# Linear attention and a two-layer network on one core: q and k transposed by half chunk, late keys against late queries only

## The chip, the core and the metric

The kernel runs on one core of a Trainium2 chip, with TensorE (PE), VectorE (DVE), ScalarE (ACT), GpSimd (POOL) and SyncE (SP), and 16 DMA engines behind the queues of SP and POOL. The metric is device time in microseconds. The kernel before was run three times: 177.3, 177.74 and 178.73 us, median 177.74.

## The reference

A decaying attention state per head, and a network of two layers behind it:

```python
# q, k, v, alpha: (4, 8, 768, 48) float32, alpha in 0.8 to 1
for t in range(S):
    state = alpha[:, :, t, :, None] * state + einsum('bhd,bhe->bhde', k[:, :, t], v[:, :, t])
    y[:, :, t] = einsum('bhd,bhde->bhe', q[:, :, t], state)
x = y.transpose(0, 2, 1, 3).reshape(B * S, H * D)        # 3072 x 384
h = x @ w_in                                             # 384 x 2048
out = square(maximum(h, 0)) @ w_out                      # 2048 x 384
```

## The kernel before

The 3072 rows are worked as 12 pairs, each of two chunks of 128 rows (256 rows; three pairs per batch). Rows lie in SBUF two to a partition: partition p of a chunk pair holds rows 2p and 2p+1 (the index `n`, or `i` in loads), so 64 partitions hold one chunk.

Attention of one pair goes in these stages.
- `loads` (L591): alpha, k, q, v, 384 KB each, by SP's queue (pair 2 by POOL's).
- `decay` (L621): logarithms of alpha on ACT, running sums over the rows by matmuls with a triangle (L637), exponentials, and the scaling of k and q by them on DVE into `qks` (L658, two instructions of 128x768). `values` (L612) casts v to bf16 into `vbf` on ACT.
- The scaled q and k are transposed into `qkt`: for pairs 0 to 3 on PE, for pairs 4 to 11 by one DMA transpose of 128 x 2048 elements (`turned_dma`, L718).
- `scores` (L759): 32 matmuls on 64x64 tiles of PE, each with 128 columns of queries, into four PSUM banks. All keys of a chunk meet all its queries; the triangle is cut out by four maskings of 128x512 on DVE into `pm` (L780).
- `carry` (L788): k times v for the state behind each chunk, 32 (or 16) small matmuls, an addition on DVE (L817), and a multiplication with the decay on POOL (L819) into `sbf`.
- For pairs 4 to 11 `mixed_back` (L897): 32 matmuls of masked scores with values (L920, 64x128 tiles, so 128 rows of output at once), and the queries with the state of before in two groups of 8 or 16 (L910, 64x64 tiles). The second waits until the first has left PE; work of another kind is put between. ACT copies the result to `yb`, and a second DMA transpose on SP (L939) makes `xt`, the network's input. Pairs 0 to 3 get `xt` from PE directly (`mixed`, L826).

The network: `up` (L953) makes 256 of the 2048 middle columns for a pair by six matmuls (L963), eight such steps a pair; ACT applies the relu (L973), DVE squares (L975). `down` (L989) has four steps of four matmuls (L996) for each chunk, then an evacuation on ACT and `store` (L942). In pairs 4 to 10 the rows come out with even and odd rows in the two halves of the partitions, and two DMAs of 64 partitions on POOL put them back for each chunk. A few matmuls on zeros (L982) fill PE while it waits at the start.

The order is not that of the code. Every step is added with a place from `TABLE` (in units of a pair's half), and `Program.order` (L147) simulates the five engines and two queues with costs given by hand, and always takes the ready instruction with the lowest place. The result is a fixed program for each engine, with waits on semaphores between them. An engine does its program in order, so one late instruction holds all behind it.

Of the kernel before, what the change touches and what calls it, by code (L numbers as in the profile page):

```python
# [16 lines left out]
    dict(decay0=-101.63878, decay1=-64.79031, turned0=-73.57009, turned1=-62.54519, scores0=-30.02735, scores1=-46.13048, carry=-24.00248, mixed=-12.61483, up=3.82089, down=9.97184, scale00=37.96521, scale01=12.07767, scale10=-55.27694, scale11=66.26176, ends=3.96969, values=3.22532, loads=-198.59615),  # L17
    dict(decay0=-62.3532, decay1=-43.34947, turned0=-42.30728, turned1=-37.91382, scores0=-25.93696, scores1=-11.6373, carry=-24.1783, mixed=3.23949, up=7.51554, down=6.63429, scale00=34.30537, scale01=-58.35352, scale10=17.21724, scale11=40.27209, ends=44.67154, values=2.77668, loads=-199.72423),
    dict(decay=-3.52293, turned=6.45487, scores0=6.82966, scores1=6.65956, carry=-0.27539, mixed=10.50945, up=12.79282, down=3.90935, loads=-64.41188),
    dict(decay=7.24503, turned=8.97861, scores0=9.08238, scores1=9.71941, carry=9.32967, mixed=10.63684, up=15.57323, down=2.06012, loads=-61.40619),  # L20
    dict(decay=7.93117, turned=8.88166, scores0=11.15836, scores1=10.85679, carry=9.32967, mixed=11.76255, up=15.22484, down=2.29842, loads=-62.88919),
    dict(decay=8.06004, turned=10.03837, scores0=11.3686, scores1=10.90735, carry=10.59388, mixed=11.41181, up=16.11414, down=1.46618, loads=5.03271),
    dict(decay=7.68334, turned=10.80342, scores0=11.5973, scores1=11.84935, carry=10.99201, mixed=14.31953, up=16.37508, down=1.46618, loads=5.21441),
    dict(decay=11.20522, turned=12.7234, scores0=13.91124, scores1=13.85916, carry=12.42083, mixed=14.21671, up=16.27226, down=1.75528, loads=11.16392),
    dict(decay=11.49025, turned=11.82737, scores0=13.75226, scores1=14.7438, carry=12.85879, mixed=15.63875, up=17.67473, down=1.71467, loads=9.89433),
    dict(decay=11.5844, turned=11.68949, scores0=14.67671, scores1=14.63718, carry=14.26836, mixed=15.50289, up=17.56635, down=1.71467, loads=9.53939),
    dict(decay=10.86409, turned=12.68953, scores0=16.09372, scores1=14.63718, carry=14.3971, mixed=11.80752, up=17.60364, down=1.71467, loads=10.75129, masks=-31.23894),
    dict(decay=10.86409, turned=12.68953, scores0=15.58331, scores1=14.80708, carry=14.3971, mixed=15.0505, up=17.60364, down=1.71467, loads=10.84157),
]
POOLS = [dict(decay=0, turned=2, scores=2, carry=1, mixed=2), dict(decay=2, turned=2, scores=1, carry=0, mixed=1)]  # L30
WEIGHTS = (-75.69063, -62.43345)
TURNED = (0, 1, 2, 3)
BACK = (4, 5, 6, 7, 8, 9, 10, 11)
BEHIND = {6: 4, 7: 6, 8: 6, 9: 7, 10: 7, 11: 9}
RUNS = {10: 16}
WARMUP = (28, 1)
WIDE = 0
PARTS = ((1, 3, 6), (2, -1, 3))
OPENS = {3: 7}
QUEUED = (2,)  # L40
# [19 lines left out]
class Program:  # L60
# [26 lines left out]
    @classmethod  # L87
    def kind(cls, eng, dma, nbytes):
        if dma in ("turn", "back"):
            return cls.TURN, 1000.0, 800.0, 256.0  # L90
        if dma[0] == "w":
            return 0.0, 2450.0, 1350.0, nbytes / 384.0 if dma[1] == "i" else 1536.0
        if dma[:3] == "raw":
            return cls.PAIR, 1100.0 if eng == "SP" else 2450.0, 1100.0, 350.0
        return cls.ROWS, 1000.0, 900.0, 1536.0
# [330 lines left out]
def bass_gla_recurrent__then__act_relu_squared_kernel(  # L426
# [32 lines left out]
    NY, NX = 2, 6  # L459
    NGT, NRR, NOS = 3, 4, 8  # L460
# [13 lines left out]
    VBF = sb("vbf", [128, 2, H, PAD], BF16, NV)  # L474
    SBF = sb("sbf", [128, D + NP * PAD], BF16, NS)
# [8 lines left out]
    MASK = sb("mask", [128, 2, 2, 64], BF16)  # L484
    WIN = sb("win", [128, KT, DFF], BF16)
# [3 lines left out]
    OSB = sb("osb", [128, DM], FP32, NOS)  # L489
# [45 lines left out]
    for c in range(2):  # L535

        add("POOL", lambda g, c=c: g.affine_select(
            out=MASK[64 * c:64 * c + 64], in_=MASK[64 * c:64 * c + 64], compare_op=ALU.is_ge, fill=0.0,
            base=0, pattern=[[-1, 2], [1, 2], [2, 64]], channel_multiplier=-2),
            470, -6, reads=["mask"], writes=["mask"])  # L540
    for i in range(NQK):
# [49 lines left out]
    def loads(g, at):  # L591
        b, t0, r = g // NW, (g % NW) * TW, g % NRAW
        for j, src in ((3, alpha), (0, k), (1, q), (2, v)):
# [5 lines left out]
            if g in QUEUED:  # L599
# [11 lines left out]

    def values(g, at):  # L612
        r, vb = g % NRAW, g % NV
        dst, src = VBF[vb][:, :, :, 0:D], both(r, 2)
# [6 lines left out]
    def decay(g, at):  # L621
# [34 lines left out]
        for z in range(2):  # L656
            decays = bass.AP(tensor=ASB[a], offset=z * 2 * HD, ap=[[4 * HD, 128], [0, 2], [D, H], [1, D]])
            add("DVE", lambda dve, z=z, decays=decays: dve.tensor_tensor(  # L658
# [59 lines left out]
    def turned_dma(g, at):  # L718
        x, t = g % NQK, g % NQT
        dst = QKT[t][:].rearrange("p z i j s -> p (z i j) s")  # L720
# [37 lines left out]

    def scores(g, at, js=range(NP), late=0.0):  # L759
        t, m = g % NQT, g % NPM  # L760
        halves = sorted({j // 2 for j in js})
        banks = {(i, X): bank(POOLS[g]["scores"] if g < FIRST else 0) for X in halves for i in range(2)}

# [24 lines left out]
    def carry(g, at, spots=None):  # L788
        x, vb, c_ = g % NQK, g % NV, g % NAC
# [4 lines left out]
        def mm(pe):  # L794
            for j in range(NP):
                for n in range(2):
                    for i in range(2):
                        for c in chunks:
                            last = pe.matmul(banks[c][0][64 * i:64 * i + 64, j * D:(j + 1) * D],  # L799
                                             QKS[x][64 * c:64 * c + 64, 0, n, 2 * j + i, :],  # L800
                                             VBF[vb][64 * c:64 * c + 64, n, 2 * j + i, 0:D],
                                             start=n == 0, stop=n == 1)
            return last
        add("PE", mm, 250, at, reads=[("qks", x, 0, X) for X in range(2)] + [("vbf", vb)],
# [21 lines left out]
    def mixed(g, at, spots=None, between=None):  # L826
# [42 lines left out]
        reads = [("qkt", t, 1, X) for X in range(2)] + [("sbf", (2 * g + c) % NS) for c in chunks]  # L869
# [27 lines left out]
    def mixed_back(g, at, spots=None, between=None):  # L897

        t, m, vb, b_ = g % NQT, g % NPM, g % NV, g % NY
        banks = [pr.bank(spots or shared) for c in range(2)]  # L900
        chunks = [1] if g % NW == 0 else [0, 1]

        def before(pe, swap):
            for j in range(NP):
                for i in range(2):
                    c = i ^ swap
                    for n in range(2):
                        if c in chunks:
                            h = 2 * j + i
                            last = pe.matmul(banks[c][0][64 * n:64 * n + 64, D * h:D * h + D],  # L910
                                             QKT[t][64 * i:64 * i + 64, 1, n, j, 64 * c:64 * c + 64],
                                             SBF[(2 * g + c) % NS][64 * i:64 * i + 64, D + PAD * j:2 * D + PAD * j],
                                             start=False, stop=True, skip_group_check=True)
            return last

        def mm(pe):
            for h in range(H):
                for i in range(2):
                    for c in range(2):
                        last = pe.matmul(banks[c][0][:, D * h:D * h + D], PMB[m][64 * c:64 * c + 64, h % 2, h // 2, i, :],  # L920
# [189 lines left out]
    for g in QUEUED:  # L1110
        ahead(("weights", g - 2), [("loads", g)])
# [64 lines left out]
```

## Time and profile before

| | |
|---|---|
| profiled execution, its time | 177.66 us |
| its span on the core | 175.9 us |
| TensorE clock granted | 1.00 |
| DVE, ACT, POOL busy | 120.3, 116.8, 38.5 us |
| read from HBM, written | 25.17, 4.72 MB |
| the chain that ended last, by engine | PE 85%, DMA 9% of the span |

A group row gives line, engine, operation, tiles and shapes, the number of instructions, their busy time together and the mean of one in ns, then the engine's idle time before them and what ended it. A timeline row gives start, length and the same names. A row of a source line's view gives least, median and greatest duration in ns; the row of waits gives the total, the number of times and the longest. Matmuls are pipelined: the length of a group ends with the last matmul's end, so the distance from one group's start to the next is what it costs.

### The profile page before, as it was taken

To read this page: it belongs to the slowest core of one execution; us is meant where nothing else is said; L and a number is where in the kernel's file an instruction comes from. 1 tells how busy PE (TensorE), PEld (TensorE's weight loads), DVE (VectorE), ACT (ScalarE), POOL (GpSimd) and SP (SyncE) were. 2 spreads that over 40 slices of the span, in tenths; PEclk is the share of its full clock that TensorE was granted. 3 is DMA by queue.
4 is the path that set the end of the run, shared out by engine and by line. 5 is a ranking of instruction groups with operands and counts; after the bars stand their busy time and mean duration, and the time that the engine had idled before them with its cause. 6 is when DMAs were issued, how large, how long until landed. Compare 5 with 4: busy or idle time off the path is not lost.

```text
span 175.9 us, 5997 instructions
## 1 busy us (share of the span) xinstructions
PE 168.3 (96%) x2609; PEld 123.8 (70%) x2609; DVE 120.3 (68%) x253; ACT 116.8 (66%) x233; POOL 38.5 (22%) x68
## 2 busy tenths in 40 slices
PE   7899598999999999999999999999999999999994
PEld 7556466766778677786777777776777777777773
DVE  7887844986899899888737939877885551232220
ACT  3884458666889677489868697767675545656641
POOL 4099820100012001010222131212330302220120
PEclk9999999999999999999999999999999999999999
DMA  5999999899996994999999989999491133212222
GB/s 146 324 294 173 203 338 221 140 276 246 318 321 100 307 304 101 148 315 201 324 201 319 238 159 296 195 321 173 100 182 32 22 71 60 56 22 48 45 45 91
DMA packets 76314, 32.89 MB, mean 187 GB/s; under 512 B 69632, under 2 KB 75456, under 8 KB 76288
## 3 DMA queue, kind: packets, MB, share of 16 engines
q1 hardware_dynamic: 70384, 25.04, 61.4%
q0 software_dynamic: 5904, 7.47, 20.7%
q8 instruction: 20, 0.33, 0.8%
q14 instruction: 6, 0.05, 0.1%
HBM read 25.17 MB, written 4.72 MB: 170 GB/s over the span
## 4 chain that ended last, share of the span: by engine, by line
PE 85%; DMA 9%; POOL 2%; ACT 1%; DVE 1%; issue 1%
PE psO L996 34%; PE psH L963 33%; DMA win<-in_moe_w_in_dram 6%; DMA xt<-yb 3%; PE psG L770 3%; PE psO L982 2%; PE psG L920 2%; POOL win L574 2%; PE psG L799 2%; PE psG L838 2%; PE psO L1015 2%; PE psG L910 1%; PE psG L710 1%; PE psG L637 1%; DVE qks L691 1%; ACT asb L688 1%
## 5 line engine op out<-in xcount | busy, mean ns | idle before, releaser
L973 ACT ACTIVATE rr<-psH 128x512 bf16<-128x512 f32 x96 | 58.2, 611 | 37.6 <-PE psH L963 36.5
L963 PE MATMUL psH<-xt,win 128*128 128x256 bf16 x576 | 75.8, 273 | 2.5 <-DMA win<-in_moe_w_in_dram 2.1
L996 PE MATMUL psO<-wout,gt 128*128 128x384 bf16 x368 | 71.5, 326 | 0.7 <-ACT xt L879 0.7
L975 DVE TENSOR_TENSOR gt<-rr 128x512 bf16<-128x512 bf16 x96 | 41.4, 439 | 38.4 <-ACT rr L973 37.9
L963 PEld LDWEIGHTS psH<-xt,win 128*128 128x128 bf16 x576 | 54.0, 98 | 16.1 <-ACT rr L973 3.1
L996 PEld LDWEIGHTS psO<-wout,gt 128*128 128x128 bf16 x368 | 35.0, 98 | 17.3 <-ACT xt L879 0.9
L949 POOL DMA_DIRECT2D out_dram<-osb x28 | 15.1, 544 | 71.3 <-ACT osb L1003 71.0
L780 DVE TENSOR_TENSOR pm<-psG,mask 128x512 bf16<-128x512 f32 x45 | 28.7, 682 | 1.8 <-PE psG L770 0.6
L819 POOL TENSOR_TENSOR sbf<-ust,acp 128x192 bf16<-128x192 f32 x16 | 9.3, 580 | 52.4 <-DVE ust L817 52.3
L658 DVE TENSOR_TENSOR qks<-raw,asb 128x768 bf16<-128x768 f32 x20 | 18.3, 951 | 3.2 <-ACT asb L647 3.2
L1003 ACT ACTIVATE osb<-psO 128x384 f32<-128x384 f32 x23 | 11.4, 494 | 3.7 <-PE psO L996 3.2
L647 ACT ACTIVATE asb<-psG 128x384 bf16<-128x384 f32 x20 | 9.8, 492 | 2.9 <-PE psG L639 2.6
L627 DVE TENSOR_TENSOR raw<-raw 128x384 f32<-128x384 f32 x20 | 11.0, 564 | 0.1
L770 PEld LDWEIGHTS psG<-qkt 64*64 64x64 bf16 x360 | 6.0, 106 | 4.3 <-issue 2.7
L770 PE MATMUL psG<-qkt 64*64 64x128 bf16 x360 | 8.7, 220 | 0.1
L619 ACT ACTIVATE vbf<-raw 128x768 bf16<-128x768 f32 x10 | 8.5, 853 | 0.2 <-DMA raw<-in_v_dram 0.2
L936 ACT ACTIVATE yb<-psG 128x384 bf16<-128x384 f32 x14 | 6.4, 490 | 2.5 <-PE psG L910 1.8
L982 PE MATMUL psO<-warm 128*128 128x128 bf16 (+1 forms) x39 | 7.0, 343 | 1.1 <-DVE warm L518 1.1
L817 DVE TENSOR_TENSOR ust<-psG,sbf 128x192 f32<-128x192 f32 x15 | 5.3, 353 | 2.5 <-PE psG L799 1.4
L627 DVE TENSOR_TENSOR raw<-raw,ro 128x384 f32<-128x384 f32 x10 | 6.1, 612 | 0.2 <-DMA raw<-in_q_dram 0.2
L643 ACT ACTIVATE ro<-raw 128x384 f32<-128x384 f32 x10 | 5.2, 518 | 0.4 <-DMA raw<-in_alpha_dram 0.4
L633 ACT ACTIVATE lab<-raw 128x384 bf16<-128x384 f32 x10 | 5.2, 524 | 0.2 <-DVE raw L627 0.2
(98 smaller groups left out, 131.0 us busy)
## 6 DMA issues: line engine op xcount, KB each, us to landing
raw<-in_alpha_dram SPq DMA_DIRECT2D x11, 384.0 KB, 4.7
raw<-in_k_dram SPq DMA_DIRECT2D x11, 384.0 KB, 4.8
raw<-in_q_dram SPq DMA_DIRECT2D x11, 384.0 KB, 4.8
raw<-in_v_dram SPq DMA_DIRECT2D x11, 384.0 KB, 5.6
out_dram<-osb POOLq DMA_DIRECT2D x28, 96.0 KB, 3.3
out_dram<-osb SPq DMA_DIRECT2D x9, 192.0 KB, 4.3
wout<-in_moe_w_out_dram POOLq DMA_DIRECT2D x4, 384.0 KB, 14.3
win<-in_moe_w_in_dram POOLq DMA_DIRECT2D x3, 384.0 KB, 9.5
```

The source lines that it names most:

```text
L627: add("DVE", lambda e: e.tensor_tensor(dst, a0, a1, ALU.mult), 470, at_, reads=reads, writes=writes, port=True)
L647: add("ACT", lambda act, z=z: act.activation(ASB[a][:, z, 0, :], ps[:, 0:HD], AF.Exp, scale=2.0 * z - 1.0), 372, at + 0.04 + 0.02 * z, rea ...
L658: add("DVE", lambda dve, z=z, decays=decays: dve.tensor_tensor(QKS[x][:, z, :, :, 0:D], both(r, z), decays, ALU.mult), 870, at + 0.05 + 0. ...
L770: last = pe.matmul(banks[i, j // 2][0][64 * c:64 * c + 64, col:col + 128].rearrange("p (a b) -> p a b", a=2), QKT[t][64 * i:64 * i + 64, 0 ...
L780: add("DVE", lambda dve, i=i, X=X, ps=ps: dve.tensor_tensor(PMB[m][:, i, 2 * X:2 * X + 2].rearrange("p j n s -> p j (n s)"), ps[:].rearran ...
L949: add(by, lambda e, dst=dst, ps=ps: e.dma_start(dst, OSB[o][ps, :]), 600, at + 0.01 * i, reads=[("osb", o)], dma=("own" if by == "POOL" el ...
L963: last = pe.matmul(ps[:, f * TW:(f + 1) * TW].rearrange("p (c t) -> p c t", c=2), WIN[:, kt, fj * 128:(fj + 1) * 128], XT[:, 2 * (g % NX): ...
L973: add("ACT", lambda act: act.activation(ro, ri, AF.Relu), 480, at, reads=[key], writes=[key, ("rr", r)])
L975: add("DVE", lambda dve: dve.tensor_tensor(gt[:, 2 * u:2 * u + 2, :], rr, rr, ALU.mult), 340, at, reads=[("rr", r)], writes=[("gt", g % NG ...
L982: last = pe.matmul(psO[1][:, 0:128 * wide].rearrange("p (a b) -> p a b", a=wide), WARM[:], bass.AP(tensor=WARM, offset=0, ap=[[128, 128], ...
L996: last = pe.matmul(ps[:, 0:DM], GT[g % NGT][:, fj, tt * 128:(tt + 1) * 128], WOUT[:, fj, :], start=(fj == 0), stop=(fj == FT - 1))
L1003: add("ACT", lambda act: act.activation(OSB[o][:], ps[:, 0:DM], AF.Copy), 372, at, reads=[key], writes=[key, ("osb", o)])
```

## The change

For pairs 4 to 11 (`turned_back(g)`):

- The scaling into `qks` writes another layout, with pairs of heads side by side, by four DVE instructions of 128x384 for two of 128x768.
- One DMA transpose becomes four, each of 32 partitions (half a chunk) of `qks`, into a quarter of `qkt`; the four are issued one behind another on SP.
- A chunk of 128 rows is seen as two halves of 64, early and late. Early keys meet all 128 queries as before (16 matmuls with 128 columns), late keys meet late queries only (16 with 64 columns). The banks hold 384 columns and not 512, and the mask `maskn` has 192 columns for 256.
- v is cast to another layout, and eight DMAs a pair, issued on POOL, copy it into `vp`, half chunk by half chunk, so that 64 partitions hold the rows of one half.
- The values are used in 64x64 tiles: 48 matmuls for 32. They and the state's 32 (16 in the first pair of a batch) are dealt into two groups: `near` (early keys, half of the state's part) and `far`.
- Two chunks are stored by four DMAs of 32 partitions, for two DMAs of 64 partitions each.
- `maskn` is made once by one memset on DVE and eight selects on POOL.

Besides, `TABLE` and the other constants are new: loads of the first two pairs can be placed in three parts, the first 13 ups (`WIDE`) take turns on three PSUM banks rather than two, pair 10's joined run is put behind another down (`RUNS`), and the pools of banks for pairs 0 and 1 differ. The places of all stages move; the kinds and numbers of ups, downs, sums, carries and of all work of pairs 0 to 3 stay.

The core of the diff:

```diff
-WIDE = 0
+WIDE = 13
...
     def turned_dma(g, at):
         x, t = g % NQK, g % NQT
+        if turned_back(g):
+            for y in range(4):
+                dst = bass.AP(tensor=QKT[t], offset=512 * y, ap=[[2048, 128], [32, 16], [1, 32]])
+                src = bass.AP(tensor=QKS[x], offset=2048 * 32 * y, ap=[[2048, 32], [1, 2048]])
+                turns[g] = add("SP", lambda sp, dst=dst, src=src: sp.dma_start_transpose(dst, src), 600, at + 0.001 * y,
...
+    def copies(g, at):
...
+        for c in range(2):
+            for a in range(2):
+                for i in range(2):
+                    to = 64 * ((a + c) % 2) + 32 * i
+                    add(COPIES, lambda e, c=c, a=a, i=i, to=to: e.dma_start(
+                        vp[to:to + 32, c, :], close(g, 64 * c + 32 * a, 32, i)), 550, at + 0.01 * (4 * c + 2 * a + i),
...
+    def scores_later(g, at, halves, banks, late):
...
+                for c in range(2):
+                    for i in range(2):
+                        ps = banks[i, j // 2][0]
+                        q = bass.AP(tensor=QKT[g % NQT], offset=2048 * 64 * i + 1024 * c + 256 + 64 * j,
+                                    ap=[[2048, 64], [512, 2], [1, 64]])
+                        o = bass.AP(tensor=ps, offset=512 * 64 * c + col, ap=[[512, 64], [64 + 64 * c, 2], [1, 64]])
+                        pe.matmul(o, part(g, 0, i, j, c, 0), q)
+                for c in range(2):
+                    for i in range(2):
+                        x = col + 64 + 64 * c
+                        last = pe.matmul(banks[i, j // 2][0][64 - 64 * c:128 - 64 * c, x:x + 64],
+                                         part(g, 0, i, j, c, 1), part(g, 1, i, j, c, 1))
...
     def mixed_back(g, at, spots=None, between=None):
...
+        def block(pe, h, c, a, b):
+
+            rows, col = 64 * ((a + c) % 2), (64 + 64 * c) * b
+            return one(pe, c, b, h, within(mn, rows, 64, h % 2)[:, h // 2, col:col + 64], vp[rows:rows + 64, c, D * h:D * h + D])
...
+        def near(pe):
+            for h in range(H):
+                for b in range(2):
+                    for c in range(2):
+                        last = block(pe, h, c, 0, b)
             for j in range(NP):
-                for i in range(2):
...
+                for a in range(2):
+                    for c in chunks:
+                        last = before(pe, j, c, c, a)
             return last
...
+        def far(pe):
             for h in range(H):
...
+                for c in range(2):
+                    last = block(pe, h, c, 1, 1)
+                for c in chunks:
+                    last = before(pe, h // 2, 1 - c, c, h % 2)
             return last
```

210 lines of the change are left out of this document (150 added, 60 removed).

## The prediction

> **What bounds the kernel now.** I read the page's busy times first, then the busy time by stretch, then the tensor engine's waits, then its timeline where pairs 4 to 11 are worked.
>
> ```profile
> PE 168.3 (96%) x2609; PEld 123.8 (70%) x2609; DVE 120.3 (68%) x253; ACT 116.8 (66%) x233; POOL 38.5 (22%) x68
> 15.00:20.00 5.00, 4.59 (x67) 3.07 (x64) 4.12 (x8) 2.50 (x5) 5.00 (x8) 1.00 1.21 195
> 20.00:25.00 5.00, 3.26 (x98) 2.57 (x99) 3.01 (x6) 2.28 (x4) 1.35 (x3) 1.00 1.19 286
> 25.00:30.00 5.00, 4.22 (x62) 2.94 (x55) 2.02 (x5) 3.33 (x8) 1.09 (x2) 1.00 1.19 254
> 40.00:50.00 10.00, 10.00 (x192) 7.33 (x190) 7.62 (x15) 7.22 (x16) 0.00 (x0) 1.00 1.06 289
> 130.00:140.00 10.00, 9.71 (x129) 7.30 (x129) 6.24 (x15) 5.86 (x10) 1.11 (x3) 1.00 0.25 47
> PE psH L963 <- DMA win<-in_moe_w_in_dram: 2.1, 3, 1.5
> PE psO L996 <- ACT xt L879: 0.7, 1, 0.7
> PE psH L963 <- DMA xt<-yb: 0.3, 1, 0.3
> ```
>
> In a stretch row the first number is its length, the second PE's busy time, and the 1.00 behind POOL's the granted clock. From 40 us on PE is full (10.00 of 10.00) but for 0.29 us after 130. Before that, the three rows from 15 to 30 us leave 0.41 + 1.74 + 0.78 = 2.93 us idle, nearly all waits for the first weights and for one evacuation. So the time is PE's own work plus a start that a transfer sets. An edit pays only where it shortens PE work, or if it opens a new gap in that full stretch, costs.
>
> **The unit costs.** One pair's attention as PE runs it (start, length, line), one row of the chain (six ups in a row of others), and three groups with the mean of one matmul:
>
> ```profile
> 69.17 0.64 PE L770 MATMUL psG<-qkt 64*64 64x128 bf16 x32
> 69.74 0.83 PE L963 MATMUL psH<-xt,win 128*128 128x256 bf16 x6
> 70.41 1.46 PE L996 MATMUL psO<-wout,gt 128*128 128x384 bf16 x8
> 71.70 1.47 PE L963 MATMUL psH<-xt,win 128*128 128x256 bf16 x12
> 73.11 0.57 PE L920 MATMUL psG<-vbf,pm 64*128 64x48 bf16 x32
> 73.61 0.31 PE L910 MATMUL psG<-sbf,qkt 64*64 64x48 bf16 x16
> 73.76 0.42 PE L799 MATMUL psG<-vbf,qks 64*64 64x48 bf16 x32
> 74.01 0.32 PE L910 MATMUL psG<-sbf,qkt 64*64 64x48 bf16 x16
> 74.27 1.48 PE L963 MATMUL psH<-xt,win 128*128 128x256 bf16 x12
> 75.68 0.64 PE L770 MATMUL psG<-qkt 64*64 64x128 bf16 x32
> 65.05 0.41 PE L799 MATMUL psG<-vbf,qks 64*64 64x48 bf16 x16
> 101.63 0.66 PE psH L963 x6
> L770 PE MATMUL psG<-qkt 64*64 64x128 bf16 x360 | 8.7, 220 | 0.1
> L799 PE MATMUL psG<-vbf,qks 64*64 64x48 bf16 x304 | 5.0, 188 | 0.0
> L920 PE MATMUL psG<-vbf,pm 64*128 64x48 bf16 x224 | 4.0, 180 | 0.0
> ```
>
> A length less one matmul's own duration is the distance from first to last start. Scores: 0.64 - 0.22 = 0.42 us for 31 steps, 13.5 ns a step. Carry, with 48 columns: 0.42 - 0.19 = 0.23 us, 7.5 ns. So a small matmul on four 64x64 tiles is cheaper when fewer columns stream through it, down to some 7.5 ns.
>
> **Scores.** Each of the eight pairs keeps 32 matmuls, but 16 of them now stream 64 columns instead of 128. No row shows 64 columns; the nearest is the 48-column carry. 16 x (13.5 - 7.5) = 0.10 us a pair; no gain is the other bound, if the mixed order doesn't pipeline. I take 0.10, as 64 is much nearer to 48 than to 128.
>
> **Values and the state's part.** Before: 0.50 us from the first L920 to the first L910, then two groups of 16 at about 7.8 ns, 0.25 us: 0.75 us, and the exits, which stay. After: 48 value blocks and 32 state blocks, all 64x64 with 48 columns, 80 x 7.8 ns = 0.62 us. That is 0.13 us less, though there are 16 matmuls more. The doubt is the second group: in half of its steps all four blocks write partitions 64 to 127, so only two tiles work. The row at 65.05 us has two tiles in use and takes 0.41 us for 16, as long as the 32 on four tiles. If what it shows is the limit of one tile, the second group takes 0.37 us instead of 0.25 and 0.12 of the 0.13 us is gone; if it is the limit of one half of the rows (those 16 all read the same 64 partitions, while the second group uses both halves), nothing is lost. L920 favours the second reading: with 0.57 - 0.18 = 0.39 us for 31 steps, 12.6 ns, it is no slower on two tiles that are twice as wide and use both halves. I take 0.13, with 0.01 as the other end.
>
> Sum: 8 x (0.10 + 0.13) = 1.84 us, between 0.1 us (neither gain comes) and 2.4 us (0.30 a pair, if the 16 shorter score matmuls and the change from wide to square tiles give 0.07 more).
>
> A rule of the Trainium skill speaks against this: "TensorE: Matmul & The Clock Gate", section "Wait — 56ns, not 53.3ns?", says that start-to-start never drops below about 25 ns however few columns there are. By that the 16 extra matmuls cost 0.4 us a pair. The trace disagrees: 7.5 ns in the carry row above.
>
> **Changes of tile shape.** Going between 128x128 and tiled work costs about 0.1 us each way: the 12 ups before the values take from 71.70 to 73.11, 1.41 us, where twice the 0.66 us of six is 1.32. The built order has 28 tiled visits after the first up where it had 27: +0.2 us.
>
> **The start.** The built order puts the second half of pair 1's scores ahead of the first up, and gives the first 13 ups a third bank. Before the last input weights land, PE has the same work to choose from, so the wait of 2.1 us moves rather than goes. Eight small selects for the new mask stand on POOL, seven ahead of a cast, one ahead of the weight loads:
>
> ```profile
> L616 POOL CAST vbf<-raw 128x768 bf16<-128x768 f32 x2 | 1.7, 862 | 4.8 <-DVE qks L691 4.8
> L525 POOL TENSOR_SCALAR_AFFINE_SELECT hinc<-hinc 128x128 bf16<-128x128 bf16 x1 | 0.3, 292 | 0.9 <-DVE hinc L523 0.9
> ```
>
> Seven times at most 0.29 us fit into the 4.8 us that the cast waits; the eighth delays the weights by up to 0.3 us. Against it stands the 0.7 us wait of L996 on an evacuated bank, which the third bank and other pools can remove. I put the start at nothing, from -1.5 to +0.5 us.
>
> **VectorE, POOL.**
>
> ```profile
> L780 DVE TENSOR_TENSOR pm<-psG,mask 128x512 bf16<-128x512 f32 x45 | 28.7, 682 | 1.8 <-PE psG L770 0.6
> L817 DVE TENSOR_TENSOR ust<-psG,sbf 128x192 f32<-128x192 f32 x15 | 5.3, 353 | 2.5 <-PE psG L799 1.4
> L658 DVE TENSOR_TENSOR qks<-raw,asb 128x768 bf16<-128x768 f32 x20 | 18.3, 951 | 3.2 <-ACT asb L647 3.2
> L691 DVE TENSOR_TENSOR qks<-raw,asb 128x384 bf16<-128x384 f32 x8 | 4.2, 552 | 0.5 <-ACT asb L688 0.5
> L949 POOL DMA_DIRECT2D out_dram<-osb x28 | 15.1, 544 | 71.3 <-ACT osb L1003 71.0
> ```
>
> A masking of 384 columns lies between 353 and 682 ns, by their slope at 550: four a pair save 0.53 us. Four scalings of 0.55 replace two of 0.95: +0.31 us. DVE is 0.2 us a pair lighter, and is no bound either way. The value copies add 8 DMA issues a pair on POOL, 64 x 0.54 = 35 us, so POOL goes from 38 to some 73 of 176 us. Behind a pair's eight issues (4.4 us) stands the multiply that makes the next state; the state is wanted by the mixing, some ten PE steps later, so I cost it at nothing, and at up to 1 us if a late ACT cast holds POOL's queue.
>
> **SyncE and the transposes.** This is where the change can lose.
>
> ```profile
> L722 SPq DMA_TRANSPOSE qkt<-qks x8: 1427/3279/3967, 54.2 to 126.6; - x8
> DMA to landing us min/median/max: 4.9/6.3/7.7
> L939 SPq DMA_TRANSPOSE xt<-yb x8: 1211/1327/3314, 66.9 to 147.2; - x8
> 126.60 2.66 SPq L722 DMA_TRANSPOSE qkt<-qks  x1
> 129.36 1.26 SPq L939 DMA_TRANSPOSE xt<-yb  x1
> 129.36 5.34 DMA xt<-yb
> ```
>
> One transpose that moves 512 KB takes SP 1.43 to 3.97 us; the smaller one, of the output, never under 1.21. Four quarters should take 4 x 1.21 = 4.84 us, 1.56 over the median, and the last lands as much later (estimate: 6.3 + 1.6 = 7.9 us). Against that the built order gives more room. Counted in ups and downs of four or six matmuls (0.65 us), there are 12, 13 and 12 between a pair's sums and its scores for pairs 4, 5 and 6 before, and 16, 20 and 17 after; the least for any of the eight goes from 12 to 14, 1.3 us more. So most of the delay is covered, and I cost it at nothing, with the bound below in the first rival. Data moved by the copies (0.2 MB a pair) and by the larger number of DMAs lies in a stretch where SP stands waiting part of the time.
>
> The profiled execution took 177.66 us, the median of the runs 177.74, so the sum needs no correction: 177.66 - 1.84 + 0.2 = 176.0 us.
>
> **The rivals.**
> *The queue of SP becomes the bound (slower).* At 126.60 a transpose of scores held SP for 2.66 us, the output transpose of pair 9 came behind it and landed 5.34 us later, and PE stood 0.25 us. After, that output transpose stands behind four quarters and a load: at least 2.2 us later (4.84 - 2.66). Pairs 4 and 10 have the same neighbourhood, with one to four quarters of the next pair ahead. If three such places each lose 1.5 us, the time is 176.0 + 4.5 = 180.5 us. It decides from some 3.6 us of new PE idle on. Against it: the wider room. The Trainium skill, "DMA: Bandwidth & Descriptors", section "Rules for kernel authors", would have small transfers coalesced, as under 64 KB mostly overhead is paid; the copies are 24 KB. No row here shows one of that size.
> *The gain is given back.* The instructions shorten but the fixed order waits instead, for masks, copies or quarters, some 0.2 us a pair: 177.7 us. For it: three waits of PE already show; against: they sum to 3 us, two thirds of it at the start.
> *The start gains too.* If half of the 2.93 us idle goes, 174.5 us.
> *Small matmuls have a floor.* If the 80 of a pair took 25 ns a step when they alternate blocks and states, 16 more cost 8 x 0.4 = 3.2 us and the time is 180.9 us. The carry row speaks plainly against it.
>
> **How the numbers follow.** The forecast has 0.46, at 176.0; its own range is 175.4 (2.4 us saved) to 177.0 (the tile limit takes 8 x 0.12 us). SP's queue 0.18, given back 0.17, start 0.15, floor 0.02, other delays 0.02. One per cent is 1.8 us, about what a measurement here can tell from no change, so 175.95 is the border. Somewhat over half of the forecast's cases lie under it (0.25), with the start 0.40 faster; the rest of it and the given-back case make 0.38; 0.22 slower. The range leaves out the floor, the upper part of SP's case and the far end of the start's: 174.0 to 179.4.
>
> **What would show it.** Right: a score group of 32 under 0.56 us from first to last end, a mixing without the gap between its two shapes, PE full from 40 us on, a mean masking of some 550 ns, the four quarters' issue near 1.2 us each. Wrong: PE waiting on the transposed q and k or on the transposed output in the middle of the span (the first rival), a second value group longer than the first per matmul (the tile limit), first ups later than 17 us (the start), or POOL's multiply held behind copies and DVE's state sum waiting on it.

## The result, and the profile after

The changed kernel takes 188.38 us (median of four runs, 186.45 to 189.24), the kernel before 177.52: 1.059 times as long, 95% interval 1.049 to 1.069. Forecast were 176.0 us, with a range up to 179.4. Times and ratios here leave out the few runs that lay more than 1.5% above the fastest of their kernel. The profiled execution took 188.35 us, 10.7 more than the 177.66 of before, and its span is 186.6 us against 175.9.

From the page, the busy times and the chain that ended last:

```profile
PE 169.5 (91%) x2741; PEld 124.6 (67%) x2741; DVE 117.7 (63%) x270; ACT 115.0 (62%) x233; POOL 73.8 (40%) x140
PE 57%; DMA 14%; DVE 9%; SPq 8%; POOL 3%; ACT 3%; issue 3%; POOLq 0%
```

PE works about as long as before (168.3 us), but only 57% of the chain is PE, where it was 85%. DMA, SP's own issuing (SPq) and DVE have come in. The next two fences are the busy time by stretch (length, then PE's busy time) and PE's waits from 40 us on:

```profile
40.00:180.00 140.00, 132.00 (x2164) 1.00 0.86 179
70.00:80.00 10.00, 8.07 (x190) 1.00 0.76 136
120.00:130.00 10.00, 8.18 (x172) 1.00 1.17 222
```

```profile
PE psG L849 <- DMA qkt<-qks: 5.7, 4, 2.0
PE psG L849 <- issue: 1.2, 1, 1.2
PE psO L1125 <- DVE gt L1103: 0.6, 1, 0.6
```

From 40 us on PE is idle for 8.0 us, where it was idle for 0.29. Nearly all of it (6.9 us) stands at L849, the first matmul of a pair's scores, and waits for the transposed q and k: the row without a releaser (issue) is one of these too, for it ends 0.09 us after pair 6's last quarter has landed. PE's last matmul ends at 181.4 us against 173.5 before: 7.9 us later, of which 7.7 are this idle time.

The remaining 2.8 us lie at the end. The closing line's instructions (duration three times, then the start), after and before:

```profile
L1274 POOLq DRAIN  x1: 9385/9385/9385, 177.0 to 177.0; - x1
L1274 SPq DRAIN  x1: 7/7/7, 183.6 to 183.6; - x1
```

```profile
L1125 POOLq DRAIN  x1: 4096/4096/4096, 168.2 to 168.2; - x1
```

Before the program ends each engine drains. GpSimd's drain took 4.1 us before and was over at 172.3, before PE was. Now it takes 9.4 us, from 177.0 to 186.4, and SP, which is done at 183.6, waits 2.8 us for it. No step of the prediction had a drain in it.

SP's side of the wait, from the timeline (start, length) and the view of one line; L787 is a quarter, L621 a load, L1060 the output transpose, L1077 a store:

```profile
57.66 3.12 SPq L787 DMA_TRANSPOSE qkt<-qks  x2
60.82 0.58 SPq L1077 DMA_DIRECT2D out_dram<-osb  x1
61.44 0.44 SPq L621 DMA_DIRECT2D raw<-in_k_dram  x1
61.93 0.68 SPq L621 DMA_DIRECT2D raw<-in_q_dram  x1
62.65 1.75 SPq L621 DMA_DIRECT2D raw<-in_v_dram  x1
64.52 5.71 SPq L787 DMA_TRANSPOSE qkt<-qks  x3
70.27 1.88 SPq L1060 DMA_TRANSPOSE xt<-yb  x1
72.20 1.29 SPq L787 DMA_TRANSPOSE qkt<-qks  x1
...
75.32 0.25 PE L849 MATMUL psG<-qkt 64*64 64x128 bf16 x4 [1.93 <-DMA qkt<-qks]
```

```profile
L787 SPq DMA_TRANSPOSE qkt<-qks x32: 1217/1291/3052, 53.9 to 147.4; - x32
DMA to landing us min/median/max: 2.7/4.1/7.2
```

Pair 5's q and k were scaled by 60.1 us. Its first quarter is issued at 64.5, since SP is still busy with pair 4's quarters, a store and three loads. Its fourth goes out at 72.2, behind an output transpose that held SP for 1.88 us (its input had been ready since 67.7), and lands at 75.27; PE starts 0.05 us later, after 1.93 us of idleness. Five of the eight pairs' scores start within 0.1 us of their last quarter's landing. Over the eight pairs the mean time from the last scaling to the last landing is 11.7 us, where it was 6.6 for one transpose. Half of the loss lies before the first issue, which now comes 2.8 us after the scaling instead of 0.3. Adding up SP's issues between 50 and 140 us gives 86.4 of 90 us (44.7 of them quarters), against 64.9 (23.7) before: SP had become full.

So two theories. **A**: four issues for one make the turned q and k late, and PE waits. **B**: the 64 copies of v that GpSimd issues lengthen its closing drain. Rivals: the new order of the work, or colliding transfers, open the gaps; the drain waits for the last stores. In the experiments "order kept" means that the fixed program of each engine is unchanged but for the edit.

### The profile page after: what moved, and what is told of

It is laid out like the page before. It is cut to its first block, busy times and chain, and to the rows that moved or that the text cites. A ratio compares the mean times of both kernels' runs of the same rounds, so it can differ in the third digit from the quotient of the medians.

```text
span 186.6 us, 6419 instructions
## 1 busy us (share of the span) xinstructions
PE 169.5 (91%) x2741; PEld 124.6 (67%) x2741; DVE 117.7 (63%) x270; ACT 115.0 (62%) x233; POOL 73.8 (40%) x140
## 4 chain that ended last, share of the span: by engine, by line
PE 57%; DMA 14%; DVE 9%; SPq 8%; POOL 3%; ACT 3%; issue 3%; POOLq 0%
PE psH L1091 24%; PE psO L1125 21%; SPq L787 7%; DMA qkt<-qks 6%; DMA win<-in_moe_w_in_dram 5%; DMA raw<-in_q_dram 3%; PE psG L1013 3%; DVE qks L717 2%; POOL maskn L553 2%; PE psO L1144 1%; PE psG L946 1%; DVE gt L1103 1%; POOL win L591 1%; PE psG L849 1%; ACT rr L1101 1%
## 5 line engine op out<-in xcount | busy, mean ns | idle before, releaser
L1101 ACT ACTIVATE rr<-psH 128x512 bf16<-128x512 f32 x91 | 54.9, 612 | 31.7 <-PE psH L1091 30.1
L1091 PE MATMUL psH<-xt,win 128*128 128x256 bf16 x546 | 70.5, 273 | 1.9 <-ACT xt L987 1.2
L1103 DVE TENSOR_TENSOR gt<-rr 128x512 bf16<-128x512 bf16 x96 | 40.3, 433 | 32.2 <-ACT rr L1101 31.9
L1091 PEld LDWEIGHTS psH<-xt,win 128*128 128x128 bf16 x546 | 51.6, 98 | 13.4 <-ACT xt L987 1.5
L652 POOL DMA_DIRECT2D vp<-vbf x64 | 31.7, 504 | 21.9 <-ACT vbf L667 20.4
L860 DVE TENSOR_TENSOR pm<-psG,maskn 128x384 bf16<-128x384 f32 x32 | 15.8, 549 | 11.6 <-PE psG L853 11.6
L717 DVE TENSOR_TENSOR qks<-raw,asb 128x384 bf16<-128x384 f32 x32 | 16.8, 580 | 1.7 <-ACT asb L702 1.7
L849 PE MATMUL psG<-qkt 64*64 64x128 bf16 x128 | 4.4, 224 | 7.0 <-DMA qkt<-qks 5.7
L849 PEld LDWEIGHTS psG<-qkt 64*64 64x64 bf16 x128 | 3.1, 106 | 9.4 <-DMA qkt<-qks 7.0
L888 DVE TENSOR_TENSOR pm<-psG,mask 128x512 bf16<-128x512 f32 x13 | 8.5, 683 | 1.0 <-PE psG L878 0.8
L1013 PE MATMUL psG<-vp,pm 64*64 64x48 bf16 x336 | 6.9, 188 | 0.0
```

Source lines behind the costliest of these rows:

```text
L652: add(COPIES, lambda e, c=c, a=a, i=i, to=to: e.dma_start(vp[to:to + 32, c, :], close(g, 64 * c + 32 * a, 32, i)), 550, at + 0.01 * (4 * c ...
L717: add("DVE", lambda dve, to=to, given=both(r, z)[:, :, y:H:2], decays=decays: dve.tensor_tensor(to, given, decays, ALU.mult), 470, at + 0. ...
L860: add("DVE", lambda dve, i=i, X=X, ps=ps: dve.tensor_tensor(within(mn, 0, 128, i)[:, 2 * X:2 * X + 2, :], ps[:, 0:384].rearrange("p (j s) ...
L1013: last = pe.matmul(banks[c][0][64 * a:64 * a + 64, D * h:D * h + D], lhsT, rhs, start=(c, a) not in begun, stop=True, skip_group_check=True)
L1091: last = pe.matmul(ps[:, f * TW:(f + 1) * TW].rearrange("p (c t) -> p c t", c=2), WIN[:, kt, fj * 128:(fj + 1) * 128], XT[:, 2 * (g % NX): ...
L1101: add("ACT", lambda act: act.activation(ro, ri, AF.Relu), 480, at, reads=[key], writes=[key, ("rr", r)])
```

## The experiments

**1. Before, with its transpose in four.** L722 issues four DMAs:

```diff
-        turns[g] = add("SP", lambda sp: sp.dma_start_transpose(dst, src), 600, at,
+        def quarters(sp):
+            for y in range(4):
+                d = bass.AP(tensor=QKT[t], offset=32 * y, ap=[[2048, 128], [128, 16], [1, 32]])
+                s = bass.AP(tensor=QKS[x], offset=2048 * 32 * y, ap=[[2048, 32], [1, 2048]])
+                last = sp.dma_start_transpose(d, s)
...
+        turns[g] = add("SP", quarters, 600, at,
```

> The kernel before with its order of instructions kept as it is; only its one transpose of q and k for each of the pairs 4 to 11 is issued as four DMA transposes of 32 partitions each, at the same place of SP's program. Theory A (four issues of about 1.3 us each, one behind the other on SP, make the turned q and k late and TensorE waits for them): SP is held 5 to 7 us for a pair instead of 1.4 to 4.0, TensorE's idle time after 40 us rises from 0.3 us to 3 us or more, the waits stand at the scores and name the DMA of qkt, and the time is 181 to 187 us against 177.5. Rival (the new order of the work, not the four issues, opened the gaps): idle time below 1 us and a time within 1 us of 177.5.

Measured: 190.9 and 192.05 us against 176.92, ratio 1.081 (1.072 to 1.090). PE's waits, and its busy time and granted clock in two stretches:

```profile
PE psG L778 <- DMA qkt<-qks: 5.2, 4, 2.7
PE psH L971 <- DMA xt<-yb: 3.5, 1, 3.5
```

```profile
80.00:85.00 5.00, 4.81 (x54) 0.66 1.06 280
135.00:140.00 5.00, 2.01 (x9) 0.57 1.00 139
```

The split alone, in the old order, costs more than the whole change. The waits stand at the scores, as theory A has it, and once at the output transpose queued behind the quarters, for 3.5 us, which is the place that the prediction's first rival named. The time is above the expected 187: PE was idle for 9.6 us after 40 us, and around the long waits the granted clock fell, which the expectation had not priced (in the two stretches shown 5 x 0.34 + 5 x 0.43 = 3.9 us; more on this below).

**2. After, with one transpose for a pair.** The first of the four moves all, the others are not issued:

```diff
-                dst = bass.AP(tensor=QKT[t], offset=512 * y, ap=[[2048, 128], [32, 16], [1, 32]])
-                src = bass.AP(tensor=QKS[x], offset=2048 * 32 * y, ap=[[2048, 32], [1, 2048]])
+                dst = QKT[t][:].rearrange("p z i j s -> p (z i j) s")
+                src = QKS[x][:].rearrange("p z i h d -> p (z i h d)")
...
         for op in self.programs[e]:
+            if op.dma in ("turn1", "turn2", "turn3"):
+                continue
```

> The changed kernel with its order kept; the first of a pair's four transposes moves the whole pair in one DMA into the same tile, the other three are left out, and the scores and the mixing read the tile at the places where they read it before. The columns then stand in another order, so q and k are mismatched and the output is not the reference's; every other instruction, wait and shape stays. Theory A: the waits on the DMA of qkt go (5.7 us in the trace of the changed kernel), TensorE's idle time after 40 us falls from 8.0 to under 2 us, its last matmul ends at about 175 instead of 181.4 us, and with the same 2.8 us of closing drain the time is 181 to 183 us. Rival (the waits come from transfers that collide, the copies and loads, whatever the number of issues): idle time stays above 6 us and the time at 187 or more.

Measured: 181.32 us, ratio 1.025 (1.018 to 1.031); 7 us of the loss are gone. No wait on qkt is left among PE's, its last matmul ends at 174.3, and the drain (9387 ns, from 170.0) ends the program. The transposes:

```profile
L790 SPq DMA_TRANSPOSE qkt<-qks x8: 1945/4098/5621, 52.9 to 135.4; - x8
DMA to landing us min/median/max: 5.0/8.1/9.3
```

One whole transpose holds SP for 4.1 us in the median where the four quarters of a pair hold it for 6.4 in the mean, and it lands after 8.1 us, slower than the 6.3 us of before. What ended the waits is thus the earlier start, on a freer SP, as much as the shorter flight. Theory A holds, by undoing (2) and by doing alone (1). With the order kept and 2.0 us of idle time left, the new order of the work is not what opens the gaps.

**3. After, without the copies.** The 64 copies are not issued, the mixing reads the tile that they would have read:

```diff
+            if op.dma is not None and op.dma[:2] == "vp":
+                continue
...
-            return one(pe, c, b, h, within(mn, rows, 64, h % 2)[:, h // 2, col:col + 64], vp[rows:rows + 64, c, D * h:D * h + D])
+            return one(pe, c, b, h, within(mn, rows, 64, h % 2)[:, h // 2, col:col + 64], bass.AP(
+                tensor=VBF[g % NV], offset=2 * H * PAD * rows + HD * c + D * h, ap=[[2 * H * PAD, 64], [1, D]]))
```

> The changed kernel with its order kept and the 64 DMA copies of v on GpSimd left out; the mixing reads v from the tile that the copies read, at addresses of the same shape, so v is in the order of the tokens and the output is not the reference's. Theory B (GpSimd's closing drain takes about 0.05 us for each DMA that the engine issued, so the 64 copies make it 9.4 instead of 4.1 us and it ends last): the drain falls to about 4 to 6 us, the end of the span follows TensorE's last matmul by about 2.3 us instead of 5.2, TensorE's idle time stays at about 8 us, and the time is 185 to 186 us. Rival (the copies' packets delay the transposes): TensorE's idle time after 40 us falls below 4 us, and the time to 181 or less. Rival (the drain waits for the last stores): drain and time unchanged.

```profile
L1291 POOLq DRAIN  x1: 4297/4297/4297, 173.8 to 173.8; - x1
```

Measured: 182.25 us, ratio 1.028 (1.023 to 1.034). The drain shrinks as theory B says. (The copies' semaphores are still there, so their number is not the cause; and the expectation's 0.05 us a DMA was too little for its own numbers, which give 5.3 us for 64.) But the gain of 6 us is twice what the drain is worth: PE's idle time after 40 us is 4.9 us and not the expected 8, and its last matmul ends at 178.1, 3.3 us earlier. Either the copies delay the transposes too, or chips differ, so it was repeated beside the changed kernel (10).

**4. After, with GpSimd's last eight stores on SP.**

```diff
+        late = self.programs["POOL"][-8:]
...
+        self.programs["POOL"] = self.programs["POOL"][:-8]
+        self.programs["SP"][-3:-3] = late
```

> The changed kernel with its order kept, but GpSimd's last eight DMAs, the stores of pairs 9 and 10, issued by SP ahead of its last three instructions. Theory B: GpSimd's drain still takes 8 us or more, since 97 DMAs of its own are left, but it begins some 10 us earlier and is hidden, and the time falls by about 2.8 us to 185 to 186 us; TensorE's idle time stays at 8 us. Rival (the drain's length is that of the last stores' landing): the drain shrinks to below 5 us. Rival (something else ends the span): time at 188 us.

```profile
L1283 POOLq DRAIN  x1: 9235/9235/9235, 150.7 to 150.7; - x1
```

Measured: 183.89 us, ratio 1.038 (1.031 to 1.044). The drain stays long, starts at 150.7 and is hidden; the last stores are not its cause. The gain of 4.5 us holds 1.6 us of an earlier end of PE, which lost 4.9 us idle and 1.7 at half clock (last section) and not the expected 8. The moved stores come behind the waits and can't give that; the changed kernel's own runs differ by as much (186.45 to 189.24 us).

**5. Before, with 64 idle copies on GpSimd.** Eight behind the last decay step of each of pairs 3 to 10:

```diff
+    def copies(eng, k):
+        for x in range(8):
+            p, c = 32 * (x % 4), x // 4
+            eng.dma_start(EXTRA[p:p + 32, k, c, :], SRC[p:p + 32, :]).then_inc(extra_sems[x], 16)
```

> The kernel before with its order kept, and 64 more DMA copies on GpSimd: after the last decay step of each of the pairs 3 to 10 eight copies of 32 partitions from one unused tile to another, 384 B for each partition, that nothing waits for but the end. Theory B (the closing drain grows with the number of copies that GpSimd issued): the drain grows from 4.1 to about 9.4 us, starts where it did, at about 168 us, and ends at about 177.6, behind SP's last wait at 175.7; the time rises by about 2 us, to 178.5 to 179.5, with TensorE's idle time after 40 us still below 1 us. Rival (the drain's length comes from the stores in four parts or from the number of semaphores): drain 4 to 5 us and time within 1 us of the kernel before. Rival (the copies' packets delay the loads and transposes): TensorE's idle time above 2 us.

```profile
L1143 POOLq DRAIN  x1: 9277/9277/9277, 167.9 to 167.9; - x1
```

Measured: 179.94 us against 177.4, ratio 1.017 (1.010 to 1.024): the drain alone, put into the kernel before, costs about what theory B says, if a little more than the expected 179.5. PE is idle for 0.8 us after 40 us, once for a transpose (0.7): here too the transposes' median hold on SP rises, from 3.28 to 3.70 us. From 4096 to 9277 ns is 81 ns a copy, though these move half the bytes of the change's. The eight stores of experiment 4 took only 150 ns off, 19 ns each. So it does not go by the number of DMAs alone, as the theory had it; why a copy within SBUF weighs more was not tried.

**6. After, planned anew with a quarter's measured price.**

```diff
-            return cls.TURN, 1000.0, 800.0, 256.0
+            return cls.TURN, 1000.0, (2500.0 if nbytes == 128 * 1024 else 800.0), 256.0
...
-                turns[g] = add("SP", lambda sp, dst=dst, src=src: sp.dma_start_transpose(dst, src), 600, at + 0.001 * y,
+                turns[g] = add("SP", lambda sp, dst=dst, src=src: sp.dma_start_transpose(dst, src), 1290, at + 0.001 * y,
```

> The changed kernel, planned anew with one correction: a quarter's transpose is told to the planner with 1290 ns on SP instead of 600, and with 2500 ns of landing instead of 800, as the trace of the changed kernel shows it. Theory A with an order that can mend it: the scores are placed later or the transposes earlier, TensorE's idle time after 40 us falls from 8.0 to under 3 us, and the time with the unchanged closing drain is 182 to 185 us. Rival (SP has too much to issue between 50 and 140 us, 96% of the time in the changed kernel, for any order to help): idle time stays above 5 us and the time at 186 or more.

Measured: 196.77 us, ratio 1.110 (1.098 to 1.122): a miss, the slowest of all. PE is idle for 10.7 us after 40 us and ran at half clock in three stretches of 3.4 us. Its longest waits are no longer for the transposes but for the logarithms (`lab`) of the decays:

```profile
PE psG L692 <- ACT lab L688: 3.8, 2, 2.2
```

So the new plan did harm in several places. SP's timeline shows one that bears on theory A:

```profile
63.10 3.98 SPq L787 DMA_TRANSPOSE qkt<-qks  x2
72.55 1.22 SPq L1060 DMA_TRANSPOSE xt<-yb  x1
73.81 2.61 SPq L787 DMA_TRANSPOSE qkt<-qks  x2
```

Two of pair 5's quarters went out, then SP stood from 67.1 to 72.5 us at an output transpose that the plan had put between them, until `yb` was written, and the other two waited behind it: 18.3 us passed from pair 5's scaling to its last landing. PE had other work meanwhile, so what this place cost is not shown. A truer price in the plan did not help where the plan may part what is wanted together.

**7. One transpose, and the late stores on SP** (2 and 4 together).

> The second and the fourth experiment in one: the changed kernel with its order kept, one transpose for a pair in place of four (columns in another order, so the output is not the reference's), and the last eight stores of GpSimd on SP. If theories A and B are the whole loss: TensorE ends at about 174.3 us as in the second experiment, the drain is hidden, and the time is 178 to 179 us, within 1.5% of the kernel before; what is left of the change then gains nothing. Rival (the end is held by something else too): 180 us or more. Rival (scores and mixing do gain once the waits are gone): 176 us or less.

Measured: 179.24 us, ratio 1.012 (1.007 to 1.017). It is a little above the expected 179; PE still stood 1.7 us in waits with no releaser shown, which are gone in experiment 12, without the copies.

**8. After, with the second value group spread over four tiles.**

```diff
                 for c in range(2):
-                    last = block(pe, h, c, 1, 1)
+                    last = block(pe, h, c, 1, 1, h // 2 % 2)
...
```

The new argument names the half of the output's partitions.

> The changed kernel, but in the second group of the mixing the blocks of late keys and late queries of every other two heads are summed into the other half of the output's partitions, so that each of the four 64x64 tiles gets 8 matmuls there instead of 12, 12, 4 and 4; the output is not the reference's. If one tile's turn of about 31 ns is the limit, the second group falls from 0.37 us to about 0.25 us for a pair. Rival (the rate at which the engine takes instructions and weights is the limit): it stays at 0.37 us.

The mixing of pair 7: in the changed kernel the first row of the first group, the first row of the second (its 32 matmuls are broken into many rows) and what follows it; then the last two in the experiment.

```profile
108.01 0.44 PE L1013 MATMUL psG<-vp,pm 64*64 64x48 bf16 x32
...
108.67 0.21 PE L1013 MATMUL psG<-vp,pm 64*64 64x48 bf16 x2
...
109.16 0.34 PE L1125 MATMUL psO<-wout,gt 128*128 128x384 bf16 x1
```

```profile
105.55 0.21 PE L1014 MATMUL psG<-vp,pm 64*64 64x48 bf16 x2
...
105.93 0.34 PE L1126 MATMUL psO<-wout,gt 128*128 128x384 bf16 x1
```

From the second group's start to the next work it was 0.49 us and is 0.38. From first to last start the 32 matmuls take 0.37 us in the changed kernel and 0.27 to 0.31 in the six pairs here that have 32 (the two first pairs of a batch have 24). The tile that gets 12 matmuls sets the time, at 31 ns each. A limit of one half of the output's partitions would fit this run too (24 of the 32 write one half in the changed kernel, 16 here), but not the prediction's row at 65.05 us: its 16 matmuls on two tiles write 8 to each half and still take 0.22 us. In one run the kernel took 186.99 us.

**9 and 10. The changed kernel again, and without copies, on one chip.**

> The changed kernel again, unaltered, so that it and the next run share a chip. Each of its runs so far had TensorE's last matmul between 179.8 and 181.4 us and a time of 186.5 to 189.2 us. If the copies play a part in the waits, this run and the next differ by more than the 2.8 us of the closing drain; if not, by that alone.

> The third experiment again (the 64 copies of v left out, so the output is not the reference's), beside the changed kernel on one chip. If the copies' packets delay the transposes: 5 us or more below the changed kernel, with TensorE's last matmul at least 2 us earlier. Rival (only the drain is theirs, and the third experiment's further gain was the spread between chips and runs): 2 to 4 us below it, TensorE's last matmul within 1 us.

Measured: 188.27 us, ratio 1.063 (1.055 to 1.072), and 182.02 us, ratio 1.027 (1.018 to 1.035), with PE's last matmul ending at 180.9 and 178.6 us. PE's longest waits with the copies, then without:

```profile
PE psG L849 <- DMA qkt<-qks: 5.1, 3, 3.0
PE psG L849 <- ACT rr L1101: 1.1, 1, 1.1
```

```profile
PE psG L708 <- ACT lab L704: 2.5, 1, 2.5
PE psG L865 <- issue: 1.5, 1, 1.5
```

The copies cost some 6 us: 2.8 in the drain, and most of the rest in PE's waits. The idle time after 40 us falls from 7.6 to 4.0 us, but behind the wait of 2.5 us the second kernel ran at half clock for 3.4 us, which gives 1.7 us back; its last matmul comes 2.3 us earlier.

**11. After, planned anew with the four transposes as one entry, late stores on SP.**

```diff
+            def quarters(sp):
+                for y in range(4):
...
+            turns[g] = add("SP", quarters, 5200, at, reads=[("qks", x, z, X) for z in range(2) for X in range(2)],
...
-            store("POOL" if turned_back(g) and g < G - 1 else "SP", o, n, at)
+            store("POOL" if turned_back(g) and g < G - 3 else "SP", o, n, at)
```

> The changed kernel planned anew with a pair's four transposes as one entry of the plan, 5200 ns on SP and 4500 ns of landing, so that nothing can be placed between them, and with the stores of pairs 8, 9 and 10 on SP. Theory A as the sixth experiment left it (four issues are dear, and dearer where SP's order puts a waiting output transpose between them): TensorE's idle time after 40 us falls below 4 us and, with the drain hidden, the time is 179 to 183 us. Rival (SP is too full for any order): 185 us or more.

```profile
PE psG L1017 <- DVE pm L864: 3.0, 2, 2.6
PE psH L1095 <- ACT rr L1105: 1.3, 3, 0.7
PE psG L853 <- DMA qkt<-qks: 0.5, 2, 0.3
```

Measured: 185.86 us, ratio 1.050 (1.044 to 1.057). That lies above the expected 179 to 183 and 2 us above experiment 4, which hides the drain too; the idle time after 40 us is 5.5 us. The scores wait only 0.5 us now, and PE waits for the masked scores (`pm`) instead, 2.55 us of it before pair 8's mixing. But this is the same lateness one step on: pair 8's last quarter landed at 114.80 us, 16.2 us after the scaling, its scores began 0.14 us later, and their masks were ready at 118.0. Neither order that was planned with the truer prices (6 and 11) recovers what four issues cost; a hand-made one was not tried.

**12. One transpose, and no copies** (2 and 3 together).

> The second and the third experiment in one: the changed kernel with its order kept, one transpose for a pair in place of four, and no copies of v (columns and rows in another order, so the output is not the reference's). What is left of the change is its gain on TensorE: scores and mixing in the new tiles, the masks, the layout, the new order. If the prediction's sum of TensorE's work holds, 1.84 us less 0.2 us, the time is about 1.6 us below the kernel before, 175 to 176 us. If, as the traces of the two kernels show, only the scores gain (0.10 us a pair) and the mixing gives nothing, the time is within 1 us of the kernel before, 176 to 178.5 us, with TensorE idle for less than 1.5 us after 40 us.

Measured: 176.46 us against 177.04, ratio 0.998 (0.995 to 1.000). PE's busy time, and one score group with the ups behind it:

```profile
40.00:170.00 130.00, 130.00 (x2151) 1.00 0.80 178
```

```profile
62.26 0.25 PE L866 MATMUL psG<-qkt 64*64 64x128 bf16 x4
...
62.73 1.48 PE L1109 MATMUL psH<-xt,win 128*128 128x256 bf16 x12
```

PE is full from 40 to 170 us and waits for nothing, as the expectation's second case has it. With the four issues and the copies out, the loss is gone, and the time is 0.6 us lower by the medians; the interval reaches 1.000, so it can hardly be told from nothing. The transposes:

```profile
L804 SPq DMA_TRANSPOSE qkt<-qks x8: 1997/3051/4808, 52.6 to 133.7; - x8
DMA to landing us min/median/max: 4.5/5.9/8.3
```

SP's median hold for a transpose is 3.05 us here and its landing 5.9, against 4.10 and 8.1 in experiment 2, which differs by the copies alone: so the copies slow the transposes. Through what they share, the DMA engines or the queues, was not tried.

PE's idle time after 40 us, and with it what it lost at half clock, by the profiles (the experiments in brackets):

| | four transposes | one transpose |
|---|---|---|
| with the copies | 8.0, 7.6, 6.6 us (changed kernel, 9, 4) | 2.0, 1.9 us (2, 7) |
| without | 4.9, 5.7 us (3, 10) | 0.0 us (12) |

So the waits have both causes, the four issues the larger one; with neither, the new order of the work leaves PE full.

No version was found that is faster than the kernel before and computes the reference.

## Why the prediction was wrong

- **The step that failed** is the one on SyncE: "So most of the delay is covered, and I cost it at nothing". Its least price of an issue was right (1.21 us; measured 1.22 at least, 1.29 in the median), though a pair's four hold SP for 6.4 us in the mean and not 4.84. But it counted the delay as 1.6 us, the added issue of one pair, and the room as more PE steps between a pair's sums and its scores. It did not add up SP's queue: 65 of 90 us were taken already, the quarters bring it to 86, and then each pair's first quarter starts late as well. From scaling to landing a pair lost 5.1 us (11.7 less 6.6; some 1.0 to 1.4 of it go without the copies), not 1.6, against the 1.3 us of added room. Nor did it ask how much room there was: in the trace of before, four of the eight transposes landed only 1.3 to 1.7 us ahead of their scores. PE's idle time of 8.0 us is the greater part of the loss; the four issues alone, without the copies, leave 5 to 6 us of it, the copies alone 2.
- **The first rival** (0.18) had the engine and the direction, and its threshold of 3.6 us of idle time was passed. Its place was wrong: it priced the output transpose behind the quarters, while the waits came at the quarters themselves. Its 180.5 us were too few.
- **The copies at nothing, or up to 1 us**, was the second failure. The estimate looked at GpSimd's multiplications only. The copies cost 2.8 us in the drain and some 2 to 3 us in PE's waits, by slowing the transposes (experiments 9, 10 and 12). The Trainium skill's page "DMA: Bandwidth & Descriptors", section "Rules for kernel authors", which the prediction cited beside its first rival, would coalesce many small transfers into one large one, and names 64 KB as the size under which overhead prevails. The trace agrees with its direction for the copies of 24 KB, and for the quarters too, though these are 128 KB each.
- **Scores, 0.10 us a pair**: right. From the first score to the next up it was 69.74 - 69.17 = 0.57 us and is 62.73 - 62.26 = 0.47 (experiment 12).
- **Mixing, 0.13 us a pair**: wrong, the other end of 0.01 came. The prediction had named the doubt, and took the limit to be a half of the rows; it is one tile. Experiment 8 shows it: the same number of matmuls dealt evenly saves 0.1 us. From first to last start the second group takes 0.37 us in the changed kernel, as the prediction had it for that case.
- **The start at nothing**: right; pair 2's mixing, with 16 ups and eight steps of downs behind it in both kernels, starts at 40.3 us before and 40.0 after.
- **Masks at 550 ns, POOL at 73 us**: measured 549 ns and 73.8 us. **The 25 ns floor** stays refuted: the 48 matmuls of the first value group start within 0.38 us, 8 ns apart. (That rival's sum was too small by its own condition: 80 matmuls at 25 ns take 2.0 us a pair where 0.75 stood, some 10 us in all and not 3.2.)
- **The sum of PE's work**, 1.84 less 0.2 us: experiment 12, which has PE's work without the waits, gains 0.6 us by the medians. 8 x 0.10 for the scores, nothing for the mixing and 0.2 us for tile changes give the same; but the tile changes were not measured apart, and the spread of the runs is as large, so this agreement is no proof.

## What to carry to other kernels

Before splitting a DMA, add up what the issuing engine's queue already holds in that stage. Here a quarter's issue took 1.22 us at least and a whole one's 1.43, so a piece was not cheap for being small; SP, 72% busy, had no room for three more per step, and the delay grew by queueing, not by the one step's issue time. Things that are wanted together should be one entry of a plan. And copies on GpSimd had a cost at the program's end: look where its drain stands against the last store.

## What the runs showed of the hardware that was not expected

GpSimd's closing drain takes 4.1 us with 41 DMAs of loads and stores, 4.3 with the change's stores in four parts, and 9.2 to 9.4 once 64 copies within SBUF were among them, even if it starts 30 us after the last copy.

A wait of PE can cost twice. In experiment 4 PE waited 2.16 us for the scores of one pair, until 103.15 us. The rows of that stretch (length, PE's busy time), and below them that of the changed kernel's second run (experiment 9) behind a wait of 3.0 us that ended at 129.7; the third number from the end is the granted clock:

```profile
101.00:104.00 3.00, 0.85 (x35) 0.95 0.64 113
104.00:107.00 3.00, 3.00 (x14) 0.50 0.91 90
107.00:110.00 3.00, 3.00 (x111) 0.98 0.74 195
```

```profile
130.00:133.00 3.00, 3.00 (x56) 1.00 1.12 311
```

In the first, PE ran at half clock for some 3.4 us, and 3 x (0.05 + 0.50 + 0.02) = 1.7 us were lost on top of the wait; in the second, behind a longer wait, at full clock. So the length of the wait alone does not decide. The same 3.4 us at half clock came with waits of 2.5 to 2.7 us in experiments 1, 8, 10 and 11. The Trainium skill, "TensorE: Matmul & The Clock Gate", section "Part 1: The HAM clock gate", gives half clock after an idle window of about 3.4 us that runs freely; that the place in such a window matters fits the two, but 2.2 us of idleness were enough here. This goes with a wider spread between runs of a kernel that waits: the changed kernel's fastest run, 186.45 us, had a granted clock of 1.00, its slowest, 189.24, one of 0.985.
